# Moving twelve attention products behind the transposes of x, combine exponentials ahead of a score group, and a scaling ahead of two loads

## The chip, the cores and the metric

The kernel runs on one core of a Trainium2 chip. The metric is the device time of one execution in microseconds (us), lower is better. Times of parts come from one profiled execution. PE is TensorE, PEld its weight loads, DVE is VectorE, ACT is ScalarE, POOL is GpSimd and SP is SyncE.

## The reference

Attention over chunks chosen by a bound, then a soft mixture of experts with slots. Shapes: q, k, v are 4 batches x 8 heads x 768 x 64; the rows of x are 3072 x 512, with 32 slots (8 experts x 4) and 1024 hidden columns.

```python
k_chunks = k.reshape(B, H, nc, chunk, D)            # chunk = 32, nc = 24
k_min, k_max = np.min(k_chunks, axis=3), np.max(k_chunks, axis=3)
ub = np.sum(np.maximum(q * k_min, q * k_max), -1)   # per query and chunk
ub = np.where(causal, ub, -1e9)
top_chunks = np.argsort(ub, axis=-1)[..., -6:]
scores = np.matmul(q, k.T) / np.sqrt(D)
scores = np.where(selected & causal, scores, -1e9)
x = softmax(scores) @ v          # heads side by side: 3072 x 512
...
logits = x @ phi
d = softmax over all rows (logits);  slot_input = d.T @ x
slot_out[e] = np.maximum(slot_input[e] @ w1[e], 0) @ w2[e]
c = softmax over the slots (logits)
return c @ slot_out
```

## The kernel before

The 32 heads are worked as 16 pairs; pair i is batch i // 4, heads 2j and 2j + 1 with j = i % 4. The main loop (`for i in range(1, NPAIR)`) is software-pipelined by hand: iteration i computes scores and exponentials of pair i, the products with v of pair i - 1, the normalisation and the transposes of x of pair i - 2, the bound and the choice of chunks of pair i + 1, and the transposes of k and q of pair i + 2. Loads of k and q run five pairs ahead. The schedule is manual: each engine executes its instructions in the order in which the code issues them, and each helper issues work for one or two engines.

The helpers that matter here:

- `scores(i, g)` (L323, L333): one of six score groups of a pair, on PE, in 64-row tiles, the two heads side by side. It writes one of the two buffers of the PSUM pool `p_sc`, so group g needs the exponential of group g - 2 to be done.
- `expo(i, g)` (L347): the exponential of a score group, on ACT; then `mask` (L357) on POOL cuts the diagonal blocks. `GROUPS` says which blocks a group holds.
- `transposes(i, "k")` and `"q"` (L231) on PE, `evac_T` (L240) on ACT: twelve small transposes into a buffer of the PSUM pool `p_tp`, then one copy to SBUF.
- `pv(i, ts)` (L375): exponentials times v for the row blocks `ts`, on PE. Row block t takes t + 1 products for each head, so `[0, 1, 2]` are twelve, `[3]` eight, `[4]` ten and `[5]` twelve. All six blocks of a pair go into the one buffer of `p_at`, which `normalise` (L387, L388, DVE) of the pair before must have read.
- `x_transposes(i)` (L397): six transposes of a pair's normalised x, on PE, into a buffer of `p_tp`; `evac_x` (L408) copies them out on DVE.
- `ubound` (L275, L282, PE), `select` (L294, L297, DVE, and a small cast on POOL), `ns_transposes` (L305, PE) and `evac_ns` (L313, DVE): the bound, the choice of chunks, and its transposition, which the scores of the next pair add as a mask.

`p_tp` has two buffers for all transposes, bounds and small products. Which of the two a tile gets is settled when the program is built, by which one is released first in the code's order.

Every fourth iteration also does the slot work of a batch: `moe_logits` at the end of i = 5, 9, 13, and in i = 6, 10, 14 (`slots` is true) `moe_exp` (L449 on PE, L454 or L456 on DVE, L458 and L465 on POOL), `moe_exp2` (L470, L473 on ACT), `moe_scale` (L477 on POOL: the running slot sums `si_acc` are rescaled; not for the first batch), `moe_comb` and `moe_comb2` (`exp_c`, L494, L497, L498 on ACT: the combine weights), `moe_dispatch` (L509, L513 on PE; L516 or L518 to L527 on DVE) and `moe_ct` (L532 on PE, L540 on DVE: the combine weights transposed). The last batch's slot work, the experts and the output follow after the loop.

Around the change the order of an iteration is:

```python
scores 0, expo 0, scores 1, expo 1, ubound(i+1), normalise(i-2), select(i+1)
transposes(i+2, "k"), evac_T
pv(i-1, [0, 1, 2])
scores 2, expo 2, scores 3, expo 3
x_transposes(i-2)
pv(i-1, [3]), transposes(i+2, "q"), evac_T, ...
scores 4, expo 4, scores 5, expo 5, ns_transposes(i+1), pv(i-1, [4]), pv(i-1, [5]), ...
```

Of the kernel before, what the change touches and what calls it, by code (L numbers as in the profile page):

```python
# [59 lines left out]
def kernel(  # L60
# [76 lines left out]
    def load_w(i):  # L137

        if i < E:
            src = moe_w1[i].rearrange("(a p x) f -> p a (x f)", p=P, x=2)  # L140
            dst = w_sb[i].rearrange("p (a f) -> p a f", a=NDG // 2)
        else:
            src = moe_w2[LATE[i - E]].rearrange("(a p x) d -> p a (x d)", p=P, x=4)
            dst = w_sb[i].rearrange("p (a f) -> p a f", a=NFG // 4)
        nc.gpsimd.dma_start(out=dst, in_=src)  # L145

    def load(i, nm):

        b, j = divmod(i, NPB)
        t = ring[nm][i % 5]  # L150
        src = {"k": k, "q": q}[nm][b, 2 * j:2 * j + 2]
        nc.gpsimd.dma_start(out=t, in_=src.rearrange("h (p g) d -> p h (g d)", p=P))  # L152
        st[nm, i] = t
# [162 lines left out]
    def scores(i, g):  # L316
        ps = p_sc.tile([P, 2, 512], F32, name="sc_ps", tag="sc")
        kT, qT, nsT = st["kT", i], st["qT", i], st["nsT", i]
        for kg, q0, w, c in (GROUPS_LAST if i == LAST else GROUPS)[g]:
            qs = slice(kg * P + q0, kg * P + q0 + w)  # L320
            for h in range(2):
                r = slice(h * 64, (h + 1) * 64)
                nc.tensor.matmul(  # L323
                    ps[:, h, c:c + w], lhsT=kT[r, kg * P:(kg + 1) * P], rhs=qT[r, qs],
                    start=True, stop=False,
                )
            t0, t1 = kg + q0 // P, kg + (q0 + w) // P
            runs = [(x, max(t0, x * NJ), min(t1, (x + 1) * NJ)) for x in range(2)]
            runs = [r for r in runs if r[1] < r[2]]
            for x, f, l in runs:  # L330
                for h in range(2):
                    r = slice(h * 64, (h + 1) * 64)
                    nc.tensor.matmul(  # L333
                        ps[:, h, c + (f - t0) * P:c + (l - t0) * P],
                        lhsT=smask[r, x, kg].rearrange("p a b -> p (a b)"),
                        rhs=nsT[r, (f - x * NJ) * P:(l - x * NJ) * P], start=False, stop=(l == t1),
                    )
        st["scps", i, g] = ps

    def expo(i, g, masked=True):  # L340
        pieces = (GROUPS_LAST if i == LAST else GROUPS)[g]
        w = sum(x[2] for x in pieces)
        if w == 512:
            e = ep.tile([P, 2, 512], BF16, name="e_sb", tag="e_sb")
        else:
            e = ep3.tile([P, 2, 384], BF16, name="e3_sb", tag="e3_sb")
        nc.scalar.activation(e[:, :, :w], st.pop(("scps", i, g))[:, :, :w], func=ACT.Exp, scale=scale)  # L347

        st["e", i, g] = e
        if masked:  # L350
            mask(i, g)
# [10 lines left out]
    def pv(i, ts):  # L362
        if i == LAST and ts[0] == 0:
            st["at", i] = p_tp.tile([P, 2, 3 * (D + 1)], F32, name="at_ps", tag="tp")
        elif i == LAST and ts[0] == 3:
            st["at", i] = p_sc.tile([P, 2, 512], F32, name="at_ps", tag="sc")
        elif ts[0] == 0:
            st["at", i] = p_at.tile([P, 2, 512], F32, name="at_ps", tag="at")
        at, tb = st["at", i], 3 if i == LAST and ts[0] > 2 else 0
        for t in ts:  # L370
            for h in range(2):
                o = at[:, h, (t - tb) * (D + 1):(t - tb + 1) * (D + 1)]
                for kg in range(t + 1):
                    g, c = (BLOCK_LAST if i == LAST else BLOCK)[(kg, t)]
                    nc.tensor.matmul(  # L375
                        o, lhsT=st["e", i, g][:, h, c:c + P], rhs=v_t[i % NV][:, h, kg, :],
                        start=(kg == 0), stop=(kg == t),
                    )

    def normalise(i, t0=0, t1=NQT, at=None):  # L380
        b, j = divmod(i, NPB)
        at = st.pop(("at", i)) if at is None else at
        at = at[:, :, :(t1 - t0) * (D + 1)].rearrange("p h (t d) -> p h t d", t=t1 - t0)
        if j == 0:
            st["x", b] = xp.tile([P, NQT, H, D], BF16, name="x_sb", tag="x_sb")
        inv = tp2.tile([P, 2, NQT, 1], F32, name="inv", tag="inv")[:, :, t0:t1]
        nc.vector.reciprocal(inv, at[:, :, :, D:D + 1])  # L387
        nc.vector.tensor_tensor(  # L388
            st["x", b][:, t0:t1, 2 * j:2 * j + 2, :].rearrange("p t h d -> p h t d"),
            at[:, :, :, :D], inv.broadcast_to([P, 2, t1 - t0, D]), op=ALU.mult,  # L390
        )

    def x_transposes(i, t0=0, t1=NQT):
        b, j = divmod(i, NPB)
        ps = p_tp.tile([P, NQT, P], BF16, name="xT_ps", tag="tp")
        for t in range(t0, t1):
            nc.tensor.matmul(  # L397
                ps[:, t, :], lhsT=st["x", b][:, t, 2 * j:2 * j + 2, :].rearrange("p h d -> p (h d)"),
                rhs=ident, is_transpose=True,
            )  # L400
        if j == 0:
            st["xT", b] = xtp.tile([P, NPB, S], BF16, name="xT_sb", tag="xT_sb")
        st["xTps", i, t0] = ps
# [139 lines left out]
    def have(i):  # L543
        return 0 <= i < NPAIR

    def moe(step, i):

        if have(i) and i % NPB == NPB - 1:
            step(i // NPB)
# [5 lines left out]
    def weights(i):  # L555
        nonlocal nw
        for _ in range(wplan.get(i, 0)):
            load_w(nw)
            nw += 1
# [58 lines left out]
    for i in range(1, NPAIR):  # L618
        slots = have(i - 3) and (i - 3) % NPB == NPB - 1
        if i >= EARLY:  # L620
            wt = ctx.enter_context(tc.tile_pool(name=f"wt{i}", bufs=1))
            w_sb.append(wt.tile([P, NFG * Dm], BF16, name=f"w_sb{i}"))
            weights(i)
        if have(i + 5) and not slots:
            load(i + 5, "k")
            load(i + 5, "q")
        scores(i, 0)
        expo(i, 0)
        moe(moe_max, i - 3)
        scores(i, 1)  # L630
        expo(i, 1)
        if have(i + 1):
            ubound(i + 1)
        moe(moe_bound, i - 3)
        if have(i - 2):
            normalise(i - 2)
        if i == LAST:
            moe_ct_copy(B - 2)
        if have(i + 1):
            select(i + 1)  # L640
        moe(moe_comb, i - 3)
        if have(i + 2):
            transposes(i + 2, "k")
            evac_T(i + 2, "k")
        if not slots:
            if have(i + 2):
                load_v(i + 2)
            if i < EARLY:
                weights(i)
        pv(i - 1, [0, 1, 2])  # L650
        for g in (2, 3):
            scores(i, g)
            expo(i, g, not slots)
        moe(moe_exp, i - 3)
        if slots:
            mask(i, 2)
            mask(i, 3)
        if have(i + 5) and slots:
            load(i + 5, "k")
            load(i + 5, "q")  # L660
        if have(i - 2):
            x_transposes(i - 2)
        pv(i - 1, [3] if i < LAST else [3, 4])
        if have(i + 2):
            transposes(i + 2, "q")
            evac_T(i + 2, "q")
            kmin(i + 2)
        moe(moe_exp2, i - 3)
        if have(i - 2):
            evac_x(i - 2)  # L670
        if have(i + 2):
            kmax(i + 2)
        moe(moe_scale, i - 3)
        if slots:
            if have(i + 2):
                load_v(i + 2)
            if i < EARLY:
                weights(i)
        scores(i, 4)
        expo(i, 4)  # L680
        if i == LAST:
            pv(i - 1, [5])
        moe(moe_comb2, i - 3)
        scores(i, 5)
        expo(i, 5)
        if have(i + 1):
            ns_transposes(i + 1)
            evac_ns(i + 1)
        if i < LAST:
            pv(i - 1, [4])  # L690
        moe(moe_dispatch, i - 3)
        if i < LAST:
            pv(i - 1, [5])
        if have(i + 2):
            qsplit(i + 2)
        moe(moe_ct, i - 3)
        moe(moe_logits, i - 2)
        moe(moe_copy, i - 2)
        if i == LAST - 2:
            l_ctx.close()  # L700
        if i == LAST - 1:
            u_ctx.close()
# [293 lines left out]
```

## Time and profile before

| | us |
|---|---|
| median of 3 runs | 161.91 (160.84 to 162.04) |
| the profiled execution | 161.03 |
| its span | 159.3 |
| busy: PE / PEld / DVE / ACT / POOL | 137.7 / 93.6 / 122.7 / 122.1 / 103.0 |

The span reaches from the first to the last instruction of the profiled execution; the rest of its time lies around it. Matmuls are pipelined, so that one starts while the one before it still runs, and the ends of matmuls are modelled. In a timeline a row gives the start, the duration, the engine, the line of the kernel, the operation, output and inputs, the size, how many instructions the row merges, and in brackets the idle time before it and what ended it. In the list of waits a row gives who waited for whom, the total, how many times, and the longest.

### The profile page before, as it was taken

The numbers are of one execution on the slowest core, as the hardware profiler recorded it, in microseconds if no ns is written. First come the engines' busy times: TensorE is split into PE (matmuls) and PEld (weight loads), VectorE is DVE, ScalarE is ACT, GpSimd is POOL, SyncE is SP. The second block draws the span as 40 slices with busy tenths as digits, with TensorE's granted clock in tenths as the row PEclk, the third lists the DMA queues.
The fourth block names the chain that finished last, engine by engine and source line by source line (L and its number), as shares of the span: only waits on it lengthen the run. The fifth ranks groups of instructions, "written<-read, shape, count | busy, mean of one in ns | idle before, by whom it ended". The sixth has DMA issues, their size and how long they took to land.

```text
span 159.3 us, 5926 instructions
## 1 busy us (share of the span) xinstructions
PE 137.7 (86%) x2435; PEld 93.6 (59%) x2436; DVE 122.7 (77%) x436; ACT 122.1 (77%) x168; POOL 103.0 (65%) x201
## 2 busy tenths in 40 slices
PE   7796779999999998999999989999898999978400
PEld 5473446767667776767777766767667854433000
DVE  5367889999999998999999699999952751287620
ACT  3288879999999898999989889998788632076510
POOL 6979779599797679888766976759574710000000
PEclk9999999999999999999999999999999999999965
DMA  2999999999999999999999999999999999239996
GB/s 39 149 179 202 190 208 206 185 203 205 182 208 198 202 207 200 204 183 207 198 203 203 202 203 204 201 207 194 210 203 214 215 214 200 60 116 406 406 402 251
DMA packets 40571, 32.92 MB, mean 207 GB/s; under 512 B 26336, under 2 KB 34784, under 8 KB 40544
## 3 DMA queue, kind: packets, MB, share of 16 engines
q0 software_dynamic: 38384, 26.25, 110.6%
q1 hardware_dynamic: 2160, 6.29, 10.1%
q8 instruction: 19, 0.31, 0.7%
q14 instruction: 8, 0.07, 0.1%
HBM read 52.49 MB, written 6.29 MB: 369 GB/s over the span
## 4 chain that ended last, share of the span: by engine, by line
PE 48%; ACT 17%; DVE 12%; DMA 8%; issue 6%; POOL 4%; DVEq 0%; ACTq 0%; SPq 0%; POOLq 0%
ACT e_sb L347 11%; PE sc_ps L323 9%; PE at_ps L375 8%; PE sc_ps L333 6%; DMA out_dram<-o_sb 5%; PE tr_ps L231 5%; PE xT_ps L397 4%; ACT qT L240 4%; DMA q_in<-in_q_dram 3%; DVE x_sb L388 3%; PE h_ps L834 2%; PE ub_ps L282 2%; PE ub_ps L275 1%; DVE mx L294 1%; PE so_ps L873 1%
## 5 line engine op out<-in xcount | busy, mean ns | idle before, releaser
L347 ACT ACTIVATE e_sb<-sc_ps 128x1024 bf16<-128x1024 f32 (+1 forms) x96 | 83.1, 917 | 6.6 <-PE sc_ps L333 6.0
L357 POOL TENSOR_SCALAR_AFFINE_SELECT e_sb<-e_sb 128x256 bf16<-128x256 bf16 x96 | 39.8, 437 | 12.0 <-ACT e_sb L347 11.6
L323 PE MATMUL sc_ps<-qT,kT 64*128 64x384 bf16 (+3 forms) x258 | 36.8, 306 | 2.6 <-ACT e_sb L347 1.7
L333 PE MATMUL sc_ps<-nsT,smask 64*128 64x384 bf16 (+2 forms) x294 | 38.1, 284 | 0.1
L375 PE MATMUL at_ps<-v_t,e_sb 128*128 128x65 bf16 x642 | 28.4, 194 | 1.6 <-DVE x_sb L388 1.4
L375 PEld LDWEIGHTS <-e_sb 128*128 128x128 bf16 x642 | 24.5, 98 | 3.8 <-issue 2.5
L323 PEld LDWEIGHTS <-kT 64*128 64x128 bf16 x258 | 13.9, 93 | 10.7 <-issue 5.3
L294 DVE MAX8 mx<-ub_ps 128x8 f32<-128x8 f32 (+1 forms) x192 | 16.8, 162 | 4.0 <-PE ub_ps L282 3.8
L162 POOL DMA_DIRECT2D v_t<-in_v_dram x16 | 16.6, 1040 | 3.4 <-PE xT_ps L397 1.4
L249 DVE TENSOR_REDUCE mm<-kT 128x24 bf16<-128x768 bf16 x16 | 15.1, 943 | 3.1 <-ACT kT L240 3.1
L333 PEld LDWEIGHTS <-smask 64*128 64x128 bf16 x294 | 15.0, 94 | 3.8 <-issue 0.6
L240 ACT COPY kT<-tr_ps 128x768 bf16<-128x768 bf16 x16 | 12.9, 804 | 4.3 <-PE tr_ps L231 4.3
L388 DVE TENSOR_TENSOR x_sb<-at_ps,inv 128x768 bf16<-128x768 f32 (+1 forms) x17 | 15.5, 910 | 0.6
L255 DVE TENSOR_REDUCE mm<-kT 128x24 bf16<-128x768 bf16 x16 | 15.1, 943 | 0.0
L240 ACT COPY qT<-tr_ps 128x768 bf16<-128x768 bf16 x16 | 12.8, 799 | 2.8 <-PE tr_ps L231 2.8
L145 POOL DMA_DIRECT2D w_sb<-in_moe_w_dram x16 | 11.4, 714 | 1.5 <-DMA w_sb<-in_moe_w_dram 1.5
L152 POOL DMA_DIRECT2D k_in<-in_k_dram x14 | 10.2, 726 | 3.0 <-PE tr_ps L231 1.6
L152 POOL DMA_DIRECT2D q_in<-in_q_dram x14 | 10.1, 720 | 0.5 <-PE sc_ps L333 0.3
L408 DVE COPY xT_sb<-xT_ps 128x768 bf16<-128x768 bf16 (+1 forms) x15 | 8.0, 537 | 2.5 <-PE xT_ps L397 2.5
L231 PE MATMUL tr_ps<-ident,q_in 128*64 128x128 bf16 x192 | 8.4, 223 | 1.1 <-DMA q_in<-in_q_dram 0.8
L231 PE MATMUL tr_ps<-ident,k_in 128*64 128x128 bf16 x192 | 8.7, 229 | 0.2
L397 PE MATMUL xT_ps<-ident,x_sb 128*128 128x128 bf16 x96 | 8.3, 221 | 0.3 <-DVE x_sb L388 0.3
(147 smaller groups left out, 209.0 us busy)
## 6 DMA issues: line engine op xcount, KB each, us to landing
w_sb<-in_moe_w_dram POOLq DMA_DIRECT2D x16, 1024.0 KB, 15.5
out_dram<-o_sb SPq DMA_DIRECT2D x10, 512.0 KB, 4.6
v_t<-in_v_dram POOLq DMA_DIRECT2D x16, 192.0 KB, 11.6
k_in<-in_k_dram POOLq DMA_DIRECT2D x14, 192.0 KB, 10.6
q_in<-in_q_dram POOLq DMA_DIRECT2D x14, 192.0 KB, 10.9
out_dram<-o_sb SPq DMA_DIRECT2D x2, 256.0 KB, 4.1
k_in<-in_k_dram POOLq DMA_DIRECT2D x1, 384.0 KB, 7.3
q_in<-in_q_dram POOLq DMA_DIRECT2D x1, 384.0 KB, 8.4
```

The lines of the kernel that those rows point to most:

```text
L152: nc.gpsimd.dma_start(out=t, in_=src.rearrange("h (p g) d -> p h (g d)", p=P))
L162: nc.gpsimd.dma_start(out=v_t[i % NV][:, :, :, :D], in_=v[b, 2 * j:2 * j + 2].rearrange("h (g p) d -> p h g d", p=P),)
L231: nc.tensor.matmul(ps[h * 64:(h + 1) * 64, g, :], lhsT=src[:, h, g * D:(g + 1) * D], rhs=ident, is_transpose=True,)
L240: nc.scalar.copy(t.rearrange("d (p g) -> d p g", g=NQT), st.pop((nm + "ps", i)).rearrange("d g p -> d p g"),)
L249: nc.vector.tensor_reduce(mm[:, 0, 0, :], kT, axis=AX.X, op=ALU.min)
L294: nc.vector.max(mx[:, a, :], ub[:, a, :max(8, 4 * t + 4)])
L323: nc.tensor.matmul(ps[:, h, c:c + w], lhsT=kT[r, kg * P:(kg + 1) * P], rhs=qT[r, qs], start=True, stop=False,)
L333: nc.tensor.matmul(ps[:, h, c + (f - t0) * P:c + (l - t0) * P], lhsT=smask[r, x, kg].rearrange("p a b -> p (a b)"), rhs=nsT[r, (f - x * NJ ...
L347: nc.scalar.activation(e[:, :, :w], st.pop(("scps", i, g))[:, :, :w], func=ACT.Exp, scale=scale)
L357: nc.gpsimd.affine_select(out=e[:, :, c:c + P], in_=e[:, :, c:c + P], compare_op=ALU.is_ge, fill=0.0, base=0, pattern=[[0, 2], [1, P]], ch ...
L375: nc.tensor.matmul(o, lhsT=st["e", i, g][:, h, c:c + P], rhs=v_t[i % NV][:, h, kg, :], start=(kg == 0), stop=(kg == t),)
L388: nc.vector.tensor_tensor(st["x", b][:, t0:t1, 2 * j:2 * j + 2, :].rearrange("p t h d -> p h t d"), at[:, :, :, :D], inv.broadcast_to([P, ...
```

## The change

Three moves; no instruction is added or taken away.

1. In every iteration the products of the first three row blocks of pair i - 1 are issued after score groups 2 and 3 and after the transposes of x, right in front of the products of the fourth block.
2. In the iterations with slot work (6, 10, 14) the three exponentials of the combine weights are issued ahead of the fifth score group instead of behind it.
3. In iterations with slot work the loads of k and q of pair i + 5 are issued behind the rescaling of the slot sums instead of ahead of it. Both exist only in i = 10.

```diff
-        pv(i - 1, [0, 1, 2])
         for g in (2, 3):
             scores(i, g)
             expo(i, g, not slots)
         moe(moe_exp, i - 3)
         if slots:
             mask(i, 2)
             mask(i, 3)
-        if have(i + 5) and slots:
-            load(i + 5, "k")
-            load(i + 5, "q")
         if have(i - 2):
             x_transposes(i - 2)
+        pv(i - 1, [0, 1, 2])
         pv(i - 1, [3] if i < LAST else [3, 4])
...
         moe(moe_scale, i - 3)
         if slots:
+            if have(i + 5):
+                load(i + 5, "k")
+                load(i + 5, "q")
             if have(i + 2):
                 load_v(i + 2)
             if i < EARLY:
                 weights(i)
+        moe(moe_comb2, i - 3)
         scores(i, 4)
         expo(i, 4)
         if i == LAST:
             pv(i - 1, [5])
-        moe(moe_comb2, i - 3)
         scores(i, 5)
         expo(i, 5)
```

## The prediction

> **What bounds the kernel now.** I read the page first, then the waits, then the engines' timelines pair by pair. I call an iteration i after the loop variable; the copies of its transposed k and q out of PSUM are kT (pair i+2) and qT, its six exponentials E0 to E5, its score groups S0 to S5.
>
> ```profile
> span 159.3 us, 5926 instructions
> ```
>
> ```profile
> PE 137.7 (86%) x2435; PEld 93.6 (59%) x2436; DVE 122.7 (77%) x436; ACT 122.1 (77%) x168; POOL 103.0 (65%) x201
> ```
>
> ```profile
> PE 48%; ACT 17%; DVE 12%; DMA 8%; issue 6%; POOL 4%; DVEq 0%; ACTq 0%; SPq 0%; POOLq 0%
> ```
>
> The chain lies mostly on TensorE, but 77% for ScalarE is an average that includes the expert tail. Inside the attention loop:
>
> ```profile
> 60.00:80.00 20.00, 19.29 (x374) 13.75 (x370) 19.21 (x69) 19.27 (x27) 17.59 (x32) 1.00 1.42 199
> ```
>
> After the stretch and its length come busy PE, PEld, DVE, ACT and POOL: in 20 us PE, DVE and ACT are each over 19. No engine alone is the bound; the hand-overs are. Iteration 13 on TensorE (between the two fences S2 and S3 run on without a pause), and below it on ScalarE:
>
> ```profile
> 105.74 0.55 PE L375 MATMUL at_ps<-v_t,e_sb 128*128 128x65 bf16 x12
> 106.23 0.34 PE L323 MATMUL sc_ps<-qT,kT 64*128 64x384 bf16 x2
> ```
>
> ```profile
> 106.98 0.51 PE L397 MATMUL xT_ps<-ident,x_sb 128*128 128x128 bf16 x6
> 107.33 0.42 PE L375 MATMUL at_ps<-v_t,e_sb 128*128 128x65 bf16 x8
> 107.67 0.53 PE L231 MATMUL tr_ps<-ident,q_in 128*64 128x128 bf16 x12
> ```
>
> ```profile
> 105.98 0.81 ACT L240 COPY kT<-tr_ps 128x768 bf16<-128x768 bf16 x1
> 106.83 1.51 ACT L347 ACTIVATE e_sb<-sc_ps 128x768 bf16<-128x768 f32 x2
> 108.24 0.80 ACT L240 COPY qT<-tr_ps 128x768 bf16<-128x768 bf16 x1
> ```
>
> Columns: start, duration, engine, line. The q transposes end at 107.67 + 0.53 = 108.20, qT starts at 108.24, 0.04 later, just as ScalarE comes free from E3 (106.83 + 1.51 = 108.34; its instructions overlap by 0.1). TensorE and ScalarE reach this meeting point together, with no slack. Whatever stands longer between kT and the q transposes stops ScalarE.
>
> **The products behind the transposes of x.** Nothing is added or removed: twelve L375 matmuls go from ahead of S2 to behind the six L397 ones. Their price is in a long row:
>
> ```profile
> 73.74 0.86 PE L375 MATMUL at_ps<-v_t,e_sb 128*128 128x65 bf16 x22
> ```
>
> One lasts 0.19, so 21 steps take 0.67, 0.032 each, and twelve 0.38. Ahead of S2 they took 106.23 - 105.74 = 0.49; the other 0.11 is the changeover from full-height tiles to the 64-row tiles of the scores.
>
> What the move exposes is a wait. The transposes of x write a p_tp buffer, and in the built program that buffer is, in the ordinary iterations, the one that kT has just read. So they wait for kT's end. Today that wait is covered by the twelve products: kT ends at 105.98 + 0.81 = 106.79, the transposes start at 106.98 straight behind S3. Without the products S2 and S3 come 0.49 sooner (S3 is held again until E1 has freed its buffer, about the start of kT plus 0.1), TensorE comes to the transposes too early and stands. Released by ScalarE, TensorE starts about 0.05 later:
>
> ```profile
> 60.19 0.28 ACT L494 ACTIVATE c_pad<-lc_sb 128x96 bf16<-128x96 f32 x1
> 60.36 0.36 ACT L497 ACTIVATE c_pad<-lc_sb 128x192 bf16<-128x192 f32 x1
> 60.61 0.28 ACT L498 ACTIVATE c_pad<-lc_sb 128x96 bf16<-128x96 f32 x1
> 60.79 0.81 ACT L347 ACTIVATE e_sb<-sc_ps 128x768 bf16<-128x768 f32 x1
> ```
>
> ```profile
> 60.95 0.34 PEld L532 LDWEIGHTS <-c_pad 128*128 128x128 bf16 x6 [0.26 <-ACT c_pad L498]
> ```
>
> (L498 ends at 60.89, TensorE goes on at 60.95.) The new path in iteration 13 is therefore: kT's end 106.79, + 0.05, + 0.35 for the transposes of x (107.33 - 106.98), + 0.38 for the twelve products, + 0.34 for the eight of the fourth block, + 0.53 for the transposes of q, + 0.04: qT at 108.48 instead of 108.24. Altogether 1.69 from kT's end to qT's start, where it is 1.45 now. E2 and E3 do run earlier, but they only wait in front of the same qT. Queued behind the late qT are E4, E5, and by their score buffers S0, S1, the bound and the next kT: a loop, so 0.24 is lost each time, and the loop's period grows by it from the 6.50 that lie between this kT and the one before:
>
> ```profile
> 99.48 0.81 ACT L240 COPY kT<-tr_ps 128x768 bf16<-128x768 bf16 x1
> ```
>
> The first such iteration shows the same 1.45 (29.89 to 31.34) as the last:
>
> ```profile
> 29.08 0.81 ACT L240 COPY kT<-tr_ps 128x768 bf16<-128x768 bf16 x1
> 29.93 1.51 ACT L347 ACTIVATE e_sb<-sc_ps 128x768 bf16<-128x768 f32 x2
> 31.34 0.80 ACT L240 COPY qT<-tr_ps 128x768 bf16<-128x768 bf16 x1
> ```
>
> These are i = 2 to 5, 8, 9, 12, 13: 8 x 0.24 = **+1.9 us**. Bounds of the term: -0.11 each if the transposes did not wait at all (only the changeover saved), +0.38 each if they came no earlier than now. I take the sum of the rows, 0.24.
>
> That the twelve cannot slip past the waiting transposes, iteration 7 shows: its products stood 0.39 for DVE, and the scores behind them, whose operands were long there, stood too.
>
> ```profile
> 63.81 0.54 PE L375 MATMUL at_ps<-v_t,e_sb 128*128 128x65 bf16 x12 [0.39 <-DVE x_sb L388]
> 64.28 0.34 PE L323 MATMUL sc_ps<-qT,kT 64*128 64x384 bf16 x2
> ```
>
> The Trainium skill ("TensorE: Matmul & The Clock Gate", Part 2) says the same: only weight loads are pulled ahead, matmuls stay in program order. By it the term is +0.24; were products pulled ahead, it would be the lower bound. The trace agrees (0.39 stood by all).
>
> The other iterations differ. Iterations 7 and 11 are late already, because the products wait for x_sb:
>
> ```profile
> 63.87 0.81 ACT L240 COPY kT<-tr_ps 128x768 bf16<-128x768 bf16 x1
> 64.88 1.51 ACT L347 ACTIVATE e_sb<-sc_ps 128x768 bf16<-128x768 f32 x2 [0.21 <-PE sc_ps L333]
> 66.30 0.80 ACT L240 COPY qT<-tr_ps 128x768 bf16<-128x768 bf16 x1
> ```
>
> ```profile
> 92.43 0.81 ACT L240 COPY kT<-tr_ps 128x768 bf16<-128x768 bf16 x1
> 93.82 1.51 ACT L347 ACTIVATE e_sb<-sc_ps 128x768 bf16<-128x768 f32 x2 [0.58 <-PE sc_ps L333]
> 95.23 0.80 ACT L240 COPY qT<-tr_ps 128x768 bf16<-128x768 bf16 x1
> ```
>
> kT's end to qT is 1.62 and 1.99; with 1.69 instead, +0.07 and **-0.3**. Iteration 1 has no transposes of x; it saves the changeover, -0.1. In i = 6 and 10 the transposes' buffer is released by the selection (L297), not kT. In i = 6 that ends at 56.45 + 0.46 = 56.91, and with 0.05 after it they can come only 0.1 sooner than at 57.07: +0.38 - 0.10 = +0.28 at the q transposes.
>
> ```profile
> 56.45 0.46 DVE L297 TENSOR_TENSOR ns_t<-ub_ps,mx 128x288 bf16<-128x288 f32 x1
> ```
>
> ```profile
> 57.07 0.51 PE L397 MATMUL xT_ps<-ident,x_sb 128*128 128x128 bf16 x6
> ```
>  Iteration 14 has no k or q left to transpose; by the same +0.28 its later matmuls slip. In the last iteration the products now fill the time in which S2 waits for E0:
>
> ```profile
> 119.48 0.54 PE L375 MATMUL at_ps<-v_t,e_sb 128*128 128x65 bf16 x12 [0.21 <-PE sc_ps L333]
> 119.95 0.34 PE L323 MATMUL sc_ps<-qT,kT 64*128 64x384 bf16 x2
> ```
>
> That cover is gone; they run after the transposes, and ScalarE is already waiting for what follows:
>
> ```profile
> 122.96 1.80 ACT L347 ACTIVATE e_sb<-sc_ps 128x1024 bf16<-128x1024 f32 x2 [0.74 <-PE sc_ps L333]
> ```
>
> so **+0.4**, carried into the tail.
>
> **The combine weights' exponentials ahead of E4**, in i = 6, 10, 14: the same three instructions (0.60 from 60.19 to E5 at 60.79 in i = 6), E4 later by 0.60, E5 not. E4 frees S0's buffer in the next iteration, but TensorE reaches S0 only behind the transposes of those weights, which wait today:
>
> ```profile
> PEld L532 <- ACT c_pad L498: 0.8, 3, 0.4
> ```
>
> 0.26, 0.4 and so about 0.14 in the three. These waits go, so the 0.28 from above is won back: 0, -0.1 and +0.1. If S0 did wait for the later E4, the price would be up to 3 x (0.60 - 0.27) = 1.0. The dispatch of i = 6 comes 0.28 late, and DVE stands for it already:
>
> ```profile
> 60.47 0.29 DVE L516 COPY si_acc<-si_ps 128x128 f32<-128x128 f32 x1 [0.36 <-PE si_ps L513]
> ```
>
> DVE is too full (19.21 of 20 above) to make that up before iteration 8, where S0 needs the transposed selection; 0 to 0.28 of it shows there, I take the half, 0.15. With the 0.07, i = 7 costs **+0.2**.
>
> **The slot sums' scaling ahead of two loads** acts at i = 10 alone (the first batch has no scaling, i = 14 no loads).
>
> ```profile
> DVE si_acc L518 <- POOL si_acc L477: 1.2, 1, 1.2
> ```
>
> Of this wait about half goes, and clears DVE for i = 11; that is why I let the -0.3 stand undiminished. The scaling may hold POOL for ScalarE's dm, and the k and q loads of pair 15, its v load, a weight load and two masks then issue about 0.6 late. Nobody is near them: pair 15 is first transposed three iterations on, and the masked products now stand later too. I take 0; the bounds are -0.6, half that wait, and +0.6, that delay.
>
> **Sum:** 1.9 - 0.1 + 0 + 0.2 - 0.1 - 0.3 + 0.1 + 0.4 = +2.1 us. The profiled execution took 161.03 (1.7 around its span of 159.3), 0.9 under the median of the runs, 161.91, and inside their 160.84 to 162.04. The sum makes 163.1 of it, and 164.0 of the median, which I give.
>
> **Rivals.**
>
> *Not slower, much the same.* The scores come 0.49 earlier, and ScalarE's waits for them, 0.21, 0.58 and, in iteration 14, 0.81, vanish without coming back further on. For it: all three rows stand ahead of E2. Against it: qT, and in iteration 14 the next row, do not hang on E2.
>
> ```profile
> 115.74 0.36 ACT L470 ACTIVATE d_sb<-ld 128x192 bf16<-128x192 f32 x1 [0.27 <-POOL ld L458]
> ```
>
> Price: i = 7 -0.2 instead of +0.2, i = 11 -0.6 instead of -0.3, i = 14 0.8 less: 2.1 - 0.4 - 0.3 - 0.8 = +0.6, 162.5.
>
> *Faster.* The transposes of x are not held by kT; then TensorE sets the pace and only the saved changeover counts, 14 x 0.11 = 1.5, beside the 0.3 of iteration 11: -1.8, 160.1. For it speaks TensorE's 48% of the chain; against it that kT ends only 0.19 before the transposes today, while the moved work is 0.49. The Trainium skill ("TensorEngine Tiling (Array Packing)", Key Properties) has the rule behind this rival: changing the tiling mode drains TensorE, and the change leaves out one such switch per iteration. The trace agrees that it costs something (0.11), and by that rule alone the result would be this rival's.
>
> *Slower still.* The transposes win nothing of their lead because something that ends after kT releases them, the selection say; from the point at which that end passes the present start, the full 0.38 falls on the path: 8 x 0.14 = 1.1 more, 165.1.
>
> *The second part fails*: S0 waits for the late E4, 1.0 more, 165.0.
>
> **How the numbers follow.** My case 0.52 (162.9 to 165.0), much the same 0.19, faster 0.07, slower still 0.13, second part 0.09. The range 161.9 to 165.6 leaves out the faster rival and the outer ends. A measurement of this kernel tells about 1%, 1.6 us, from no change. Of my own case 0.12 falls under that line (163.5); so faster 0.07, within 1% 0.31, slower 0.62.
>
> **What would show it.** Right: in i = 8 and 13 the L397 row shows idle before it, put down to kT; E2 follows kT without the gap, but ScalarE stands about 0.3 before qT, for PE; kT's end to qT is 1.69; the wait of L532 for c_pad is gone; DVE's 1.2 for the scaling is halved. Wrong: kT to qT stays at 1.45 or less, or the L397 row follows S3 with no idle time; the forecast falls if the loop's period does not grow from 6.5 to about 6.75 us.

## The result, and the profile after

The changed kernel takes 166.12 us (median of 6 runs, 165.44 to 166.63), the kernel before 161.06 in the same series (median of 6, 160.45 to 162.04). The ratio is 1.030, 95% interval 1.026 to 1.035: slower by 5.1 us, where 2.1 were forecast. The profiled execution took 165.75. Its page, from the head, the busy times and the chain by engine:

```profile
span 164.0 us, 5912 instructions
...
PE 137.5 (84%) x2435; PEld 93.6 (57%) x2436; DVE 124.8 (76%) x436; ACT 122.1 (74%) x168; POOL 101.9 (62%) x201
...
PE 33%; DVE 19%; DMA 16%; ACT 15%; POOL 7%; issue 5%; ACTq 0%; DVEq 0%; POOLq 0%; SPq 0%
```

PE and ACT are as busy as before (137.7 and 122.1); only DVE gained, 124.8 against 122.7. The span grew by 4.7, so the change made idle time. The chain has moved from PE (48% before) to DVE (12% before, now 19%) and to transfers. The same 20 us as before, in the table of stretches (length; PE, PEld, DVE, ACT, POOL):

```profile
60.00:80.00 20.00, 18.25 (x349) 13.02 (x348) 18.45 (x68) 18.14 (x27) 16.75 (x32) 1.00 1.42 198
```

All three engines lost about one microsecond in twenty (19.29, 19.21, 19.27 before); the granted clock (1.00) and the transfer rate (198 against 199 GB/s) did not change.

Iteration 13 is the ordinary case. PE's timeline from the last matmuls of S3 on, then ACT's:

```profile
109.95 0.34 PE L333 MATMUL sc_ps<-nsT,smask 64*128 64x384 bf16 x2
110.48 0.49 PE L397 MATMUL xT_ps<-ident,x_sb 128*128 128x128 bf16 x6 [0.19 <-ACT kT L240]
110.81 0.79 PE L375 MATMUL at_ps<-v_t,e_sb 128*128 128x65 bf16 x20
111.54 0.53 PE L231 MATMUL tr_ps<-ident,q_in 128*64 128x128 bf16 x12
```

```profile
109.62 0.81 ACT L240 COPY kT<-tr_ps 128x768 bf16<-128x768 bf16 x1
110.30 1.55 ACT L347 ACTIVATE e_sb<-sc_ps 128x768 bf16<-128x768 f32 x2
112.10 0.80 ACT L240 COPY qT<-tr_ps 128x768 bf16<-128x768 bf16 x1 [0.26 <-PE tr_ps L231]
```

The transposes of x stand 0.19 for kT and start 0.05 after its end (110.43). E2 follows kT at once, and ACT then stands 0.26 in front of qT. From kT's end to qT's start it is 1.67.

The start of kT serves as a mark for each iteration. The table gives its distance to the next kT (us), from the traces; the names stand for the runs below.

| from kT of i to the next | before | after | products alone | combine + scaling | in front of xT | masks first |
|---|---|---|---|---|---|---|
| 3 to 4, 4 to 5, 8 to 9, 12 to 13 (mean) | 6.50 | 6.73 | 6.73 | 6.50 | 6.48 | 6.73 |
| 5 to 6 / 9 to 10 | 7.06 / 7.06 | 7.28 / 7.28 | 7.64 / 7.27 | 7.05 / 7.06 | 7.03 / 7.03 | 7.28 / 7.28 |
| 6 to 7 | 8.21 | 8.19 | 8.53 | 7.90 | 8.06 | 8.16 |
| 7 to 8 | 6.68 | **7.94** | 6.72 | 7.00 | **7.63** | 6.98 |
| 10 to 11 | 8.33 | 8.43 | 8.59 | 8.29 | 8.33 | 8.42 |
| 11 to 12 | 7.04 | **7.96** | 6.75 | 7.30 | **7.96** | 7.03 |
| kT of 13 to the end | 53.32 | 54.40 | 54.41 | 53.08 | 53.35 | 54.39 |

Ordinary iterations cost 0.23 each. The two stretches behind the slot iterations cost 1.26 and 0.92, and the end 1.08. Iteration 7 in the timeline of all engines, after:

```profile
66.07 0.46 DVE L297 TENSOR_TENSOR ns_t<-ub_ps,mx 128x288 bf16<-128x288 f32 x1
66.11 0.23 POOL L296 CAST ns_t<-mx 128x12 bf16<-128x12 f32 x1 [0.94 <-DVE mx L294]
...
66.59 1.03 POOL L162 DMA_DIRECT2D v_t<-in_v_dram  x1 [0.25 <-issue]
...
67.62 0.70 POOL L145 DMA_DIRECT2D w_sb<-in_moe_w_dram  x1
...
68.32 1.49 POOL L357 TENSOR_SCALAR_AFFINE_SELECT e_sb<-e_sb 128x256 bf16<-128x256 bf16 x4
68.75 1.18 DVE L257 TENSOR_TENSOR bd<-mm,headsel 128x96 bf16<-128x96 bf16 x1
...
69.85 0.34 DVE L313 COPY nsT<-ns_ps 128x384 bf16<-128x384 bf16 x1
...
70.25 0.39 PE L333 MATMUL sc_ps<-nsT,smask 64*128 64x128 bf16 x4 [0.93 <-DVE nsT L313]
...
70.68 1.94 ACT L347 ACTIVATE e_sb<-sc_ps 128x1024 bf16<-128x1024 f32 x2 [1.10 <-PE sc_ps L333]
```

and the same place before, DVE's timeline and POOL's:

```profile
67.43 0.47 DVE L257 TENSOR_TENSOR bd<-mm,headsel 128x96 bf16<-128x96 bf16 x1
67.83 0.34 DVE L313 COPY nsT<-ns_ps 128x384 bf16<-128x384 bf16 x1
```

```profile
64.79 0.23 POOL L296 CAST ns_t<-mx 128x12 bf16<-128x12 f32 x1 [0.19 <-DVE mx L294]
...
67.00 0.78 POOL L357 TENSOR_SCALAR_AFFINE_SELECT e_sb<-e_sb 128x256 bf16<-128x256 bf16 x2
68.09 1.09 POOL L357 TENSOR_SCALAR_AFFINE_SELECT e_sb<-e_sb 128x256 bf16<-128x256 bf16 x2 [0.31 <-ACT e_sb L347]
```

L257 (a small product on DVE, 0.26 in most iterations) lasts 1.18. It ends at 69.93, 0.12 behind the end of POOL's row of masks (68.32 + 1.49 = 69.81). Before, it ended at 67.90, also 0.12 behind the end of a row (67.00 + 0.78 = 67.78), but that row had two masks, those of E2 and E3, and POOL then stood 0.31 for E4. After, the cast waits 0.94 for DVE, the v load and the weight load come next, and the masks of E2 and E3 are so late that those of E4 and E5 follow without a gap: four in a row. Behind L257 stands nsT (L313), for nsT the scores of iteration 8 (0.93), for them ACT (1.10). The list of waits sums this up:

```profile
ACT qT L240 <- PE tr_ps L231: 6.3, 15, 1.0
...
PE sc_ps L333 <- DVE nsT L313: 1.9, 2, 0.9
...
DVE si_acc L518 <- PE si_ps L513: 1.4, 2, 0.7
...
PE xT_ps L397 <- ACT kT L240: 1.1, 6, 0.2
```

The first row was 2.8 in 5 waits before: now ACT stands for the transposes of q throughout the loop. The 1.9 in two waits is new. DVE's wait of 1.2 for POOL's scaling is gone, and so is L532's for c_pad.

### The profile page after: what moved, and what is told of

It is laid out like the page before. It is cut to its first block, busy times and chain, and to the rows that moved or that the text cites. A ratio compares the mean times of both kernels' runs of the same rounds, so it can differ in the third digit from the quotient of the medians.

```text
span 164.0 us, 5912 instructions
## 1 busy us (share of the span) xinstructions
PE 137.5 (84%) x2435; PEld 93.6 (57%) x2436; DVE 124.8 (76%) x436; ACT 122.1 (74%) x168; POOL 101.9 (62%) x201
## 4 chain that ended last, share of the span: by engine, by line
PE 33%; DVE 19%; DMA 16%; ACT 15%; POOL 7%; issue 5%; ACTq 0%; DVEq 0%; POOLq 0%; SPq 0%
DMA q_in<-in_q_dram 10%; ACT e_sb L347 9%; PE at_ps L375 7%; DMA out_dram<-o_sb 5%; DVE mx L294 4%; PE xT_ps L397 4%; PE tr_ps L231 4%; PE sc_ps L323 3%; POOL e_sb L357 3%; PE sc_ps L333 3%; ACT kT L240 3%; DVE x_sb L388 2%; PE h_ps L834 2%; ACT qT L240 2%; DVE ns_t L297 2%
## 5 line engine op out<-in xcount | busy, mean ns | idle before, releaser
L357 POOL TENSOR_SCALAR_AFFINE_SELECT e_sb<-e_sb 128x256 bf16<-128x256 bf16 x96 | 38.3, 423 | 15.8 <-ACT e_sb L347 15.6
L375 PE MATMUL at_ps<-v_t,e_sb 128*128 128x65 bf16 x642 | 25.9, 194 | 0.0
L375 PEld LDWEIGHTS <-e_sb 128*128 128x128 bf16 x642 | 23.4, 98 | 0.6 <-issue 0.5
L323 PEld LDWEIGHTS <-kT 64*128 64x128 bf16 x258 | 14.8, 93 | 13.8 <-issue 7.5
L397 PE MATMUL xT_ps<-ident,x_sb 128*128 128x128 bf16 x96 | 8.1, 219 | 2.5 <-ACT kT L240 1.1
L397 PEld LDWEIGHTS <-x_sb 128*128 128x128 bf16 x96 | 6.3, 97 | 5.9 <-DVE mx L294 2.5
```

Source lines behind the costliest of these rows:

```text
L323: nc.tensor.matmul(ps[:, h, c:c + w], lhsT=kT[r, kg * P:(kg + 1) * P], rhs=qT[r, qs], start=True, stop=False,)
L357: nc.gpsimd.affine_select(out=e[:, :, c:c + P], in_=e[:, :, c:c + P], compare_op=ALU.is_ge, fill=0.0, base=0, pattern=[[0, 2], [1, P]], ch ...
L375: nc.tensor.matmul(o, lhsT=st["e", i, g][:, h, c:c + P], rhs=v_t[i % NV][:, h, kg, :], start=(kg == 0), stop=(kg == t),)
L397: nc.tensor.matmul(ps[:, t, :], lhsT=st["x", b][:, t, 2 * j:2 * j + 2, :].rearrange("p h d -> p (h d)"), rhs=ident, is_transpose=True,)
```

## The experiments

**The first move alone.** From the kernel after, the moves 2 and 3 are taken back:

```diff
+        if have(i + 5) and slots:
+            load(i + 5, "k")
+            load(i + 5, "q")
         if have(i - 2):
             x_transposes(i - 2)
...
         if slots:
-            if have(i + 5):
-                load(i + 5, "k")
-                load(i + 5, "q")
...
-        moe(moe_comb2, i - 3)
         scores(i, 4)
         expo(i, 4)
...
+        moe(moe_comb2, i - 3)
         scores(i, 5)
```

> The first move alone: the twelve products behind the transposes of x, the combine exponentials and the loads where they were. Theory A (the products, held by the transposes' wait for kT, cost 0.22 us in each ordinary iteration, and the rest of the 5 us comes from DVE running late into POOL's masks after the slot iterations): the whole loss is here, +4 to +5.5 us over the kernel before, kT's end to qT's start 1.67 us in iterations 8 and 13, and the steps from kT of iteration 7 to 8 and of 11 to 12 near 7.9 us. Rival B (the 3 us beyond the ordinary iterations come from the second and third move, which shift POOL and E4): only +1.5 to +2.5 us, those two steps near 7.0 us.

Measured: 163.97, ratio 1.016 (1.010 to 1.023), span 162.8. Theory A is wrong: only 2.7 of the 5.1 is here, and the two long stretches are gone. 7 to 8 is back at 6.72, and 11 to 12 at 6.75 lies below the 7.04 of before; 6 to 7 and 10 to 11 are 0.3 longer. The loss lies just above the rival's range, with steps shorter than its 7.0. In iteration 7 the row of masks has a gap again, and L257 ends 0.12 behind its first part:

```profile
69.04 0.48 DVE L257 TENSOR_TENSOR bd<-mm,headsel 128x96 bf16<-128x96 bf16 x1
```

```profile
68.62 0.78 POOL L357 TENSOR_SCALAR_AFFINE_SELECT e_sb<-e_sb 128x256 bf16<-128x256 bf16 x2
69.92 0.88 POOL L357 TENSOR_SCALAR_AFFINE_SELECT e_sb<-e_sb 128x256 bf16<-128x256 bf16 x2 [0.53 <-ACT e_sb L347]
```

Other collisions remain in this run. L269, half of the split of q on DVE for the bound, takes 0.35 when nothing holds it; in iteration 13 it lasts 1.29 beside a row of four masks, and the end is as long as after (54.41). In iteration 5 of this execution it lasts 1.3 too, and the step 5 to 6 takes 7.64; in the executions in which it lasts 0.67 or less there, the step is 7.28 or less.

**The moves 2 and 3 alone**, from the kernel before (with that same diff the other way round):

> The second and third move alone, the products where they were. Theory A: no loss, -0.5 to +0.3 us: the 0.8 us of TensorE's waits for c_pad go, E4 runs 0.6 us later without anyone waiting for it; DVE no longer waits 1.2 us for the scaling. Rival B: +2 to +3 us.

Measured: 161.24, ratio 1.000 (0.996 to 1.004). The wait for the combine weights is gone, as PE's weight loads of iteration 6 show, which carry no idle time now:

```profile
60.23 0.35 PEld L532 LDWEIGHTS <-c_pad 128*128 128x128 bf16 x6
```

Move 3 shows in iteration 10. First DVE before, then DVE and POOL in this run:

```profile
89.71 0.29 DVE L518 TENSOR_TENSOR si_acc<-si_acc,si_ps 128x128 f32<-128x128 f32 x1 [1.15 <-POOL si_acc L477]
...
90.76 0.34 DVE L269 TENSOR_SCALAR qpn<-qT 128x768 bf16<-128x768 bf16 x1
```

```profile
88.61 0.29 DVE L518 TENSOR_TENSOR si_acc<-si_acc,si_ps 128x128 f32<-128x128 f32 x1 [0.43 <-PE si_ps L513]
...
89.84 1.10 DVE L269 TENSOR_SCALAR qpn<-qT 128x768 bf16<-128x768 bf16 x1
```

```profile
89.72 1.03 POOL L162 DMA_DIRECT2D v_t<-in_v_dram  x1
```

The wait for the scaling is gone, and L518 starts 0.7 sooner after the start of kT. But L269 now falls beside the v load, lasts 1.10 for 0.34, and ends 0.19 behind the load: 7.21 after the start of kT (83.73) where it was 6.99 (84.11). So DVE leaves this stretch 0.2 later, not sooner. L269 is that long in iteration 10 of every run with move 3, and 0.34 in every run without it; no run has move 3 by itself.

6 to 7 shrinks by 0.31, but 7 to 8 and 11 to 12 grow by 0.32 and 0.26. So the moves cost 2.7 (first) and 0.0 (second and third) each by themselves, and 5.1 together: some 2.4 us exist only in the combination.

**The products behind S3, but in front of the transposes of x**, all else as after:

```diff
+        pv(i - 1, [0, 1, 2])
         if have(i - 2):
             x_transposes(i - 2)
-        pv(i - 1, [0, 1, 2])
```

> All three moves, but the twelve products stand between score group 3 and the transposes of x instead of behind these. Theory A: the products cover the wait for kT again, kT's end to qT's start is 1.45 us or less, E2 follows kT without a gap, the ordinary iterations take 6.5 us, and the time is that of the kernel before within 0.8 us on either side. Rival C (any place behind the scores delays the products for the iteration that follows, or crowds DVE and POOL, and that costs the 5 us): +3 us or more.

Measured: 162.70, ratio 1.010 (1.006 to 1.014). PE's timeline of iteration 13, then ACT's:

```profile
108.21 0.55 PE L375 MATMUL at_ps<-v_t,e_sb 128*128 128x65 bf16 x12
108.60 0.50 PE L397 MATMUL xT_ps<-ident,x_sb 128*128 128x128 bf16 x6
108.93 0.42 PE L375 MATMUL at_ps<-v_t,e_sb 128*128 128x65 bf16 x8
```

```profile
107.61 0.81 ACT L240 COPY kT<-tr_ps 128x768 bf16<-128x768 bf16 x1
...
109.85 0.80 ACT L240 COPY qT<-tr_ps 128x768 bf16<-128x768 bf16 x1
```

The twelve products cover the wait for kT (ending 108.42) again, and the transposes come at 108.60 with no idle time of their own; kT's end to qT is 1.43, the step 6.48. So it is the order of products and transposes that costs the 0.23, not the place of the products behind S3. The time is 1.4 above the kernel before, which neither theory gave: the ordinary iterations and the end (53.35) are as before, but 7 to 8 and 11 to 12 stay 0.95 and 0.92 too long.

**The masks first.** The kernel after, with the v load and the weight load of iterations 7 and 11 issued behind the masks of E2 and E3:

```diff
-        if not slots:
+        if not slots and i not in (7, 11):
             if have(i + 2):
                 load_v(i + 2)
...
             expo(i, g, not slots)
+        if i in (7, 11):
+            load_v(i + 2)
+            weights(i)
```

> The changed kernel, but in iterations 7 and 11 the masks of E2 and E3 stand ahead of the v load and the weight load in POOL's queue, so that POOL is not in a row of four masks when DVE comes to the small product bd (L257, 1.18 us there against 0.26). Theory A: L257 of iterations 7 and 11 takes 0.5 us or less, the transposed selection comes 0.7 us or more earlier, the steps of kT from 7 to 8 and from 11 to 12 fall from 7.95 to about 7.2 us, and the time falls by 1.0 to 1.6 us against the changed kernel (+3.4 to +4 over the one before). Rival D (DVE is late because the dispatch is late, and the collision is only a symptom): those steps fall by less than 0.2 us each.

Measured: 163.92, ratio 1.018 (1.010 to 1.025), 2.2 below after. DVE's timeline of iteration 7, then POOL's:

```profile
68.17 0.26 DVE L257 TENSOR_TENSOR bd<-mm,headsel 128x96 bf16<-128x96 bf16 x1
```

```profile
65.67 0.40 POOL L357 TENSOR_SCALAR_AFFINE_SELECT e_sb<-e_sb 128x256 bf16<-128x256 bf16 x1
66.32 0.41 POOL L357 TENSOR_SCALAR_AFFINE_SELECT e_sb<-e_sb 128x256 bf16<-128x256 bf16 x1 [0.24 <-ACT e_sb L347]
66.80 1.03 POOL L162 DMA_DIRECT2D v_t<-in_v_dram  x1
67.83 0.71 POOL L145 DMA_DIRECT2D w_sb<-in_moe_w_dram  x1
```

L257 now runs beside a load and takes 0.26; the two stretches fall by 0.96 and 0.93, which is the 0.92 and 0.93 that L257 lost. The expectation had put less on it, 1.0 to 1.6 in all and steps of about 7.2.

**The control**, the same edit in the kernel before:

> The kernel before with nothing but the masks ahead of the two loads in iterations 7 and 11. Theory A (without the moves DVE meets POOL there in a row of two masks only, L257 0.47 us): -0.3 to +0.1 us, the two steps 0 to 0.3 us shorter than 6.68 and 7.04. Rival (the order on POOL is worth about 1 us in each of them by itself, whatever stands elsewhere): -1.5 us or more.

Measured: 161.24, ratio 1.000 (0.998 to 1.003). The stretches stay at 6.68 and 7.05, though L257 falls from 0.47 to 0.26: there, the step does not hang on L257. The edit is no gain of its own; it only takes the collision out.

**The same edit with the moves 2 and 3**, to see whether L257's 0.47 is what gives their gain back:

> The second and third move alone, with the masks ahead of the two loads in iterations 7 and 11. Without the masks' change this took what the kernel before takes: the step from kT of 6 to 7 was 0.31 us shorter, those from 7 to 8 and 11 to 12 0.32 and 0.26 longer. Theory A (these are DVE's waits for POOL): the two steps fall to 6.7 and 7.0 us, and the time is 0.3 to 0.9 us under the kernel before. Rival (the gain of the second move has to be given back in any case): the time of the kernel before within 0.2 us.

Measured: 161.38, ratio 1.001 (0.998 to 1.004). The stretches are 6.99 and 7.30, as without the edit, though L257 is down to 0.26 here too: theory A is wrong, and the rival right but for its size (0.3 over the kernel before, where it allowed 0.2). Where the gain goes can be read from the traces, though no run tests it. From the start of kT in iteration 6 to the selection (L297) in iteration 7 it is 9.09 before, 9.12 with the moves 2 and 3 and 9.10 here: kT of iteration 7 comes 0.31 sooner, DVE does not. From kT of 10 to L297 of 11 it is 9.58, 9.80 and 9.86: there DVE comes later, as the longer L269 of iteration 10 would have it.

**Both cures**: products in front of the transposes of x, masks first:

> All three moves, the products between score group 3 and the transposes of x, and in iterations 7 and 11 the masks of E2 and E3 ahead of the two loads on POOL. Theory A (what is left of the loss of the earlier run with this place is the collision alone, 7.63 and 7.96 us for the steps of kT from 7 to 8 and 11 to 12): L257 takes 0.5 us or less there, the steps fall to 6.7 and 7.0 us, and the time is that of the kernel before or 0.3 to 0.8 us under it (160.4 to 161.3). Rival D (DVE is late for another reason): +1.0 us or more over the kernel before.

Measured: 161.50, ratio 1.0025 (1.0000 to 1.0049). L257 takes 0.26, and the two steps fall to 6.69 and 7.03, as expected; the time lies 0.2 above the expected range. (In this execution PE also stands 0.36 in the midst of the k transposes of iteration 9, and the step 8 to 9 takes 6.96; the profile names no engine for it.) With the two causes removed what is left of the 5.1 is 0.4, no more than this can tell from none.

**The last iteration's products in their old place**, all else as after:

```diff
+        if i == LAST:
+            pv(i - 1, [0, 1, 2])
         for g in (2, 3):
...
-        pv(i - 1, [0, 1, 2])
+        if i < LAST:
+            pv(i - 1, [0, 1, 2])
```

> The changed kernel, but in the last iteration the products stand in their old place, ahead of score group 2. Theory A (there they used to run while score group 2 waits for E0, and now stand bare): what follows kT of iteration 13 takes 0.4 to 0.6 us less than the changed kernel's 54.40 us, and E4's wait for its scores in the last iteration falls from 1.12 to about 0.75 us. Rival (the end is late for what iteration 14 hands over): less than 0.1 us.

Measured: 165.79, ratio 1.029 (1.024 to 1.034). ACT's wait in the last iteration, first after, then in this run:

```profile
127.68 1.80 ACT L347 ACTIVATE e_sb<-sc_ps 128x1024 bf16<-128x1024 f32 x2 [1.12 <-PE sc_ps L333]
```

```profile
128.07 1.80 ACT L347 ACTIVATE e_sb<-sc_ps 128x1024 bf16<-128x1024 f32 x2 [0.59 <-PE sc_ps L333]
```

kT of iteration 13 to the end falls from 54.40 to 54.04: 0.36 of the 1.08, just under what was expected. The median falls by as much (166.12 to 165.79), but the single times of the two overlap, and the span of this execution, 164.4, is even longer, because its kT of iteration 1 came 1.7 later than after (23.33 against 21.64).

**The masks first in iteration 13.** 0.23 of the 1.08 is iteration 13's own, so about half a microsecond was left. After, DVE's last L269 stands beside four masks; DVE's timeline, then POOL's:

```profile
113.78 1.29 DVE L269 TENSOR_SCALAR qpn<-qT 128x768 bf16<-128x768 bf16 x1
```

```profile
113.15 1.70 POOL L357 TENSOR_SCALAR_AFFINE_SELECT e_sb<-e_sb 128x256 bf16<-128x256 bf16 x4
```

The edit is the one of iterations 7 and 11, with `i in (13,)`. (Where the expectation speaks of four masks of E2 and E3, the row holds those of E2 to E5.)

> The kernel after, but in iteration 13 the v load and the weight load are issued behind the four masks of E2 and E3. From the start of kT in iteration 13 to the end it was 53.32 before and 54.40 after; 0.23 of the 1.08 is iteration 13's own, 0.36 was traced to the last iteration, and 0.48 is left for iteration 14. Theory A: that 0.48 is the last qpn operation (L269) of iteration 13, which lasts 1.29 instead of 0.57 beside a row of four masks. With the masks first it lasts 0.35 to 0.6, VectorE comes 0.5 sooner to iteration 14, and the stretch from kT of iteration 13 to the end falls to 53.9 (53.8 to 54.0). Rival B: iteration 14 is late because the transposes of x there stand for the selection and the products behind them; L269 does not matter, and the stretch stays at 54.3 to 54.4. All else as after, the time about 0.5 us less by A, unchanged by B.

Measured: 165.65, ratio 1.027 (1.022 to 1.031). L269 and the stretch to the end:

```profile
114.51 0.54 DVE L269 TENSOR_SCALAR qpn<-qT 128x768 bf16<-128x768 bf16 x1
```

kT of 13 to the end is 53.99, 0.41 less. The rest of iteration 14 is thus about 0.1, as forecast.

**All but the wait for kT**: the edit in 7, 11 and 13 and the last iteration's products in their old place, in one kernel.

> The kernel after with the three other losses taken out together: the masks of E2 and E3 ahead of the v load and the weight load in iterations 7, 11 and 13, and in the last iteration the first three blocks' products in their old place. What is left of the change is the wait of the transposes of x for kT in the ordinary iterations. Theory A (the losses are separate and add up): 1.9 from iterations 7 and 11, 0.48 from 13 and 0.36 from the last one come off, so 2.7 us below after, a time of 162.9 to 163.7 and a ratio of 1.010 to 1.016 to the kernel before; ordinary steps still 6.73, kT of iteration 13 to the end 53.5 to 53.6. That would be the first term of the forecast, +1.9, alone. Rival B (one loss hides another, as the collisions give back what the earlier parts won): under 2.2 us comes off, the ratio is 1.018 or more.

Measured: 163.28, ratio 1.013 (1.010 to 1.017), 2.1 above before by the medians; the span is 161.17, 1.86 above. The ordinary step is 6.73, the end 53.65, as theory A said: the losses are separate and add up. Of the 1.86 the seven ordinary iterations that can be measured (3, 4, 5, 8, 9, 12, 13) make 1.6; the step 7 to 8 keeps 0.34, what follows iteration 13 keeps 0.1, and the start is 0.2 shorter.

No version beats the kernel before; the four that equal it take 161.2 to 161.5.

## Why the prediction was wrong

The direction and the main mechanism held; the size did not. By the steps of the prediction:

- *Ordinary iterations, 8 x 0.24 = 1.9.* Right. kT's end to qT's start is 1.67 where 1.69 was worked out; the step is 6.73 for 6.75; the idle time of L397 is put down to kT, and with products in front of the transposes it goes. Seven of the eight iterations show it, 1.6 in all; that of i = 2 is lost in the varying start.
- *i = 1, -0.1.* Not to be separated. The kT of iteration 1 came 0.88 earlier than before, and by iteration 3 that was gone (35.63 against 35.60). There the chain runs through the transfers of q and POOL's queue and varies from run to run. This stays open.
- *i = 6 and 10, 0 and -0.1.* -0.02 and +0.10. The first move costs 0.32 and 0.26 there, about as put; the others win 0.31 back in i = 6 but only 0.04 in i = 10.
- *i = 7, +0.2, and i = 11, -0.3.* This is the step that failed: +1.26 and +0.92. The prediction saw that DVE comes late out of the slot work and priced that lateness at "0 to 0.28", half of it taken, as if DVE's operations kept their lengths. DVE's lag behind ACT did grow: the selection (L297) starts 1.51 after the start of kT instead of 0.88 (66.07 - 64.56 and 64.75 - 63.87). For i = 11 a premise failed besides: half of the wait for the scaling was to clear DVE. The wait went, but L269 of iteration 10 lasted 1.11 in its place beside the v load, and the selection of iteration 11 starts 9.94 after kT of 10, where it was 9.58 before and is 9.60 with the products alone. In both iterations the price came from what the lag met: POOL's cast waits for the selection, its masks close up to a row of four, and L257 waits out the row. That is 0.96 and 0.93 of the two, by the masks put first; without it, i = 11 costs nothing, and the first move alone gains the 0.29 that the prediction gave it. What remains of i = 7 and 11, 0.30 and 0.3 above that gain, is about the 0.32 and 0.26 that moves 2 and 3 lose there by themselves.
- *i = 14, +0.1.* 0.5, of which 0.41 is the same kind of collision, at L269 late in iteration 13; the rest is as forecast.
- *The last iteration, +0.4.* 0.36. Right.
- *The second part's other bound*, S0 waiting for the late E4 at up to 1.0, did not come. *The third part*: taken as 0; together with the second it measures 0.0 by itself, but it does not clear DVE, as said under i = 11.

The terms of i = 7, 11 and 14, all three set by DVE behind the slot work or the logits, were put at 0.0 together and measured 2.7; the collisions are 2.3 of it (0.96 + 0.93 + 0.41). All other terms that could be measured were within 0.2 of their sizes. The rival at 165.1 has nearly the measured time and the wrong reason: an ordinary iteration grew by 0.23, not by the full 0.38.

The lag alone does not decide whether L257 is caught: with the moves 2 and 3 alone it is 1.22 after kT's start, and L257 lasts 0.48; with the products in front of the transposes it is 1.19, and L257 lasts 1.18. It is the gap between the masks of E3 and E4 that counts. In iteration 7 E3's mask ends 3.92 after kT's start before, 4.25 with the moves 2 and 3, 4.23 with the products in front and 4.54 after; E4 ends at 4.16, 4.48, 3.99 and 4.31. In the first two POOL must stand for E4, and the row has a gap; in the last two E4 is already done, and its masks follow at once. Before, the margin is 0.24, so a small shift of either engine uses it up.

## What to carry to other kernels

Work put ahead of a wait may be what hides the wait: look at what the next instruction's buffer waits for before moving its cover behind it. Where VectorE has no slack, price a delay not by its own length but by what its next operations will then run beside; a row of GpSimd instructions without a gap can cost the length of the whole row. A wait that is taken away may come back as a longer operation (1.15 before L518, then 0.76 more in L269). And measure moves that travel together also one by one: here 2.7 and 0.0 made 5.1.

## What was not expected of the hardware

A DVE operation beside GpSimd's masks does not wait for one mask but can wait for the whole row: 0.26 alone, 0.47 beside two masks, 1.18 beside four, each time ending 0.12 after the last. The Trainium skill ("SBUF — State Buffer", sections "Who interferes with whom" and "SBUF: two separate sides") names a cause that fits: a VectorE instruction with two inputs in SBUF, as L257 has, contends with a GpSimd instruction that reads SBUF, and whichever starts first holds the shared port pair for its whole instruction. By that rule alone L257 should have lost one mask of about 0.4 at most; here the trace goes further, 0.92 lost and two mask ends passed by (four masks in 1.49 are 0.37 each, so the second and the third ended at 69.06 and 69.44). Nor is it always so: before, L269 ran in iteration 13 in 0.57 beside four masks, and after it took 1.29. What lets it in between two of them is not settled.

The loads on POOL's queue can hold a DVE operation too. They did not stretch L257 (0.26 beside the weight load in the run with the masks first), but after, L269 of iteration 10 lasts 1.11 beside the v load and ends 0.18 behind it (93.86 and 93.68). That is not always so either: before, the same L269 was done in 0.34 beside a weight load.
